# One read of w2 for two products, and V six items further behind K, in a two-block attention and MLP training step

## Chip, core and metric

The kernel runs on one core of a Trainium2 chip. The metric is the device time of one execution in microseconds (us). Engine names: PE does matmuls and transposes (PEld: its loads of the stationary operand), DVE, ACT and POOL work on vectors, SP issues the loads from memory. "arena" is the on-chip memory of the kernel, cut into twelve 1 MB slots and eight planes that hold the probabilities. For slots, blocks and slabs 1 MB is 2^20 bytes; in rates and read totals it is 10^6.

## The reference, cut to what matters

The model runs the same attention and the same MLP twice, then the gradients of all weights and of K and V are computed. There is one token, so all products with weights are matrix times vector, and the 64 MB each of K and V dominate.

```python
x = x + attn(layernorm(x), k_cache, v_cache, wq, wo)     # 32 heads, 4 KV groups, 65536 keys, 128 wide
x = x + mlp(layernorm(x), w1, b1, w2, b2)                # 1024 -> 3584 -> 1024, relu squared
x = x + attn(layernorm(x), k_cache, v_cache, wq, wo)
x = x + mlp(layernorm(x), w1, b1, w2, b2)                # its result is out_0
...                                                      # vjp: gradients of x, K, V, wq, wo, w1, b1, w2, b2
```

out_0 needs the second MLP's output product, h times w2. Nothing else in the step needs out_0: the gradients start from a given grad_out.

## The kernel before

The program has four passes over K and V and a short "dense stage" of weight products between each two of them.

| part | what it does | us in the profile before |
|---|---|---|
| first pass, second pass | attention forward: K, exponentials, V | to 374, and 424 to 773 |
| first dense stage | between them; reads w1 and w2 for the first MLP | 374 to 424 |
| second dense stage | second MLP without its output, gradient through w1 | 773 to 825 |
| third pass | gradient of the second attention, V leads and K follows | 825 to 1189 |
| third dense stage | dq to dx2 (wq), dx2 to dh2 (w2), dh2 to dx1 (w1), wo | 1189 to 1243 |
| fourth pass | gradient of the first attention, and all stores | 1243 to 2036 |

A pass goes through items of eight chunks of 128 keys, 256 items per pass. Four items are a block of 1 MB, which takes a slot. In a forward pass each step of the pipeline does K of one item and V of the item that lies FWD_LAG steps back:

```python
FWD_LAG = TLEAD + SU // 8 + 12            # 2 + 16 + 12 = 30 items
TOUCH = [touch_order(ITEMS[0], [("k", 0), ("v", FWD_LAG)]), ...]   # the order in which blocks are first needed
...
early_turn = set(k for k in TOUCH[p][:-2] if k in KV["keep"])      # V blocks turned in place for the third pass
...
pipeline(items, [(kT, 0), (kS, TLEAD), (v8, FWD_LAG)], bg, end, holds)
```

A block is loaded when it is first needed in program order; the load then waits on the chip until its slot is free.

The output product of the second MLP runs in the background of the third pass. The gradient product dx2 to dh2 reads the same w2 again in the third dense stage:

```python
bg.by_group(2, lambda g: g_dO(L3, dx3, g))
x4 = vec.tile([P, DC], F32, name="x4")
def g_out0():                              # out_0 = x3 + h @ w2 + b2, seven slabs of 1 MB
    yield from g_w2(L4, x3, x4, ps_bg)
    col_to_dram(x4, D, out_0.rearrange("a b d -> (a b d)"))
    yield
bg.add(g_out0())
... third pass ...
rows.add(PRE["wq3"], DC, R, lambda: L3["dqT"][:, gsl(lastg[2])], fin_dx2)
rows.add(w2_slabs()[0], FC, DC, lambda: dx2[:], fin_dh2, mix=True)      # w2 again
rows.add(w1_slabs()[0], DC, FC, lambda: dh2[:], fin_dx1, cols=f_cols, mix=True)
rows.add(wo_slabs(firstg[3])[0], R, DC, lambda: dx1[:], dO_finish(L1, firstg[3]))
rows.run()
```

Rows computes products whose vector runs along the rows of the stored weights. Each chunk of a slab is either turned on PE (eight transposes, L630), copied out of PSUM, and multiplied on PE (eight matmuls of 64 columns, L655), or it is multiplied and summed by one DVE instruction (L621). A balancer decides for each chunk, when the program is built, from running sums of the estimated load of PE, DVE and ACT.

## Time and profile before

The time is 2037.89 us (median of three runs, 2037.04 to 2039.66). First the profile page of the kernel before: the rate of the loads and stores in 40 slices of the span, and the bytes.

```profile
GB/s 389 424 417 418 420 423 404 362 357 420 420 418 403 419 415 278 382 419 408 421 419 421 411 334 245 370 399 424 421 418 423 391 424 400 358 392 424 424 397 247
HBM read 632.30 MB, written 165.69 MB: 392 GB/s over the span
```

In the middle of the first three passes most slices have 415 to 424 GB/s, and the deep dips there are the dense stages (slices 8 and 9, 16 and 17, 24 to 26). The Trainium skill, "Perfetto Trace Analysis", section Roofline, gives about 435 GB/s as what the 16 DMA engines of one core can move; 424 is 97% of it, and no slice of this trace goes above 424. So a byte less in a pass should be time.

The windows view of the kernel before shows the joints. The columns are the stretch in us, its length, each engine's busy us with the number of instructions, the granted PE clock, the DMA share and the rate.

```profile
core 0: us, PE busy (x) PEld busy (x) DVE busy (x) ACT busy (x) POOL busy (x), PEclk, DMA share, GB/s
745.00:774.00 29.00, 21.85 (x482) 21.15 (x479) 11.33 (x31) 19.36 (x38) 0.00 (x0) 0.88 0.82 328
1182.00:1245.00 63.00, 53.98 (x1049) 50.74 (x1045) 42.20 (x107) 34.66 (x40) 1.28 (x12) 0.92 0.86 323
1200.00:1216.70 16.70, 16.50 (x333) 15.97 (x333) 14.06 (x31) 12.43 (x14) 0.12 (x1) 0.90 0.79 289
```

The last line is the product dx2 to dh2. PE is busy for 16.50 of its 16.70 us: work added for PE here should lengthen it, unless it moves elsewhere. The granted clock of 0.90 stands for one stretch of 3.4 us at half clock inside it (1201.0 to 1204.4 us).

The PE timeline of the kernel before, at the end of the second pass (start, length, engine, line, operation, output and inputs, count, and in brackets the idle time before it with what ended it):

```profile
757.67 1.05 PE L1012 MATMUL ps_acc<-arena 128*128 128x64 bf16 x32
763.56 0.59 PE L1012 MATMUL ps_acc<-arena 128*128 128x64 bf16 x8 [4.84 <-ACT arena L993]
763.96 1.04 PE L1018 MATMUL ps_tr<-ident_b,arena 128*128 128x128 bf16 x8
```

PE has no V item left that could run and waits 4.84 us for the last exponentials. After that the eight transposes take 1.04 us. They take 0.61 us elsewhere.

The load queue of the kernel before at the start of the third pass. L330 is a single load, L335 the first load of 2 MB:

```profile
834.33 0.33 SPq L330 DMA_DIRECT2D arena<-in_A_v_cache_dram  x1
845.00 0.33 SPq L335 DMA_DIRECT2D arena<-in_A_k_cache_dram  x1
```

Nothing is issued for over 10 us. PE runs dry a little later (PE timeline, before):

```profile
853.06 0.61 PE L1147 MATMUL ps_acc<-dsT,arena 128*128 128x64 bf16 x8 [4.54 <-DMA arena<-in_A_k_cache_dram]
859.60 0.98 PE L1102 MATMUL ps_tr<-ident_b,arena 128*128 128x128 bf16 x8 [2.82 <-DMA arena<-in_A_v_cache_dram]
```

### The profile page before, as it was taken

To read this page: it belongs to the slowest core of one execution; us is meant where nothing else is said; L and a number is where in the kernel's file an instruction comes from. 1 tells how busy PE (TensorE), PEld (TensorE's weight loads), DVE (VectorE), ACT (ScalarE), POOL (GpSimd) and SP (SyncE) were. 2 spreads that over 40 slices of the span, in tenths; PEclk is the share of its full clock that TensorE was granted. 3 is DMA by queue.
4 is the path that set the end of the run, shared out by engine and by line. 5 is a ranking of instruction groups with operands and counts; after the bars stand their busy time and mean duration, and the time that the engine had idled before them with its cause. 6 is when DMAs were issued, how large, how long until landed. Compare 5 with 4: busy or idle time off the path is not lost. (4 is left out here: it accounts for less than half of the span.)

```text
span 2036.4 us, 67140 instructions
## 1 busy us (share of the span) xinstructions
PE 1630.6 (80%) x30274; PEld 1340.6 (66%) x30274; DVE 1175.9 (58%) x2355; ACT 1042.2 (51%) x1612; POOL 143.8 (7%) x328
## 2 busy tenths in 40 slices
PE   6878688688777877767777888788788888698896
PEld 6878688687777777767777786455455555455554
DVE  5645465245554644335444467577677777678675
ACT  3434344135343453235453446576676667567675
POOL 0000000000000000000000001111111111111121
PEclk9989898689998998889989999789888889789898
DMA  9999999999999997999999996999999999999996
GB/s 389 424 417 418 420 423 404 362 357 420 420 418 403 419 415 278 382 419 408 421 419 421 411 334 245 370 399 424 421 418 423 391 424 400 358 392 424 424 397 247
DMA packets 111981, 802.32 MB, mean 394 GB/s; under 512 B 9536, under 2 KB 9550, under 8 KB 49486
## 3 DMA queue, kind: packets, MB, share of 16 engines
q1 hardware_dynamic: 87646, 632.33, 76.4%
q0 software_dynamic: 24048, 165.70, 19.7%
q8 instruction: 236, 3.87, 0.7%
q14 instruction: 51, 0.42, 0.1%
HBM read 632.30 MB, written 165.69 MB: 392 GB/s over the span
## 5 line engine op out<-in xcount | busy, mean ns | idle before, releaser
L153 DVE COPY kt<-ps_tr 128x1024 bf16<-128x1024 bf16 x722 | 496.5, 689 | 455.3 <-PE ps_tr L910 223.7
L150 ACT CAST arena<-ps_gg 128x1024 bf16<-128x1024 f32 x452 | 439.8, 1010 | 220.5 <-PE ps_gg L1277 165.4
L910 PE MATMUL ps_tr<-ident_b,arena 128*128 128x128 bf16 x3840 | 310.7, 227 | 60.6 <-DMA arena<-in_A_k_cache_dram 46.6
L150 ACT COPY kt<-ps_tr 128x1024 bf16<-128x1024 bf16 x162 | 170.4, 1052 | 214.2 <-PE ps_tr L1102 152.1
L910 PEld LDWEIGHTS <-arena 128*128 128x128 bf16 x3840 | 234.2, 101 | 63.4 <-DMA arena<-in_A_k_cache_dram 49.8
L153 DVE CAST arena<-ps_gg 128x1024 bf16<-128x1024 f32 (+1 forms) x191 | 228.9, 1198 | 76.4 <-PE ps_gg L1277 42.5
L1012 PE MATMUL ps_acc<-arena 128*128 128x64 bf16 (+4 forms) x4096 | 209.5, 197 | 54.2 <-ACT arena L993 19.0
L1277 PE MATMUL ps_gg<-GG,xt 64*128 64x512 bf16 x1024 | 212.7, 414 | 42.9 <-DVE arena L153 22.2
L1223 PE MATMUL ps_tr<-ident_b,arena 128*128 128x128 bf16 x1824 | 178.1, 236 | 36.8 <-DMA arena<-in_A_v_cache_dram 36.0
L1012 PEld LDWEIGHTS <-arena 128*128 128x128 bf16 x4096 | 163.4, 101 | 59.4 <-issue 40.8
L928 PE MATMUL ps_sc<-L_qpad,kt 128*128 128x64 bf16 (+7 forms) x3584 | 183.8, 194 | 18.1 <-issue 17.9
L1102 PE MATMUL ps_tr<-ident_b,arena 128*128 128x128 bf16 x1888 | 157.0, 231 | 46.7 <-DMA arena<-in_A_v_cache_dram 44.9
L993 ACT ACTIVATE arena<-S_sb,L_negm 128x128 bf16<-128x128 f32 x256 | 165.1, 1002 | 55.1 <-DVE L_negm L978 45.9
L1223 PEld LDWEIGHTS <-arena 128*128 128x128 bf16 x1824 | 120.4, 105 | 93.1 <-issue 52.6
L928 PEld LDWEIGHTS <-kt 128*128 128x128 bf16 x3584 | 153.4, 100 | 21.0 <-issue 18.6
L1102 PEld LDWEIGHTS <-arena 128*128 128x128 bf16 x1888 | 119.2, 103 | 51.4 <-DMA arena<-in_A_v_cache_dram 48.0
L1303 PE MATMUL ps_acc<-X,arena 128*128 128x64 bf16 (+3 forms) x2048 | 121.3, 200 | 24.6 <-DMA arena<-in_A_k_cache_dram 24.6
L1303 PEld LDWEIGHTS <-arena 128*128 128x128 bf16 x2048 | 88.5, 103 | 60.0 <-issue 33.5
L993 ACT ACTIVATION_READ_ACCUMULATOR arena<-S_sb,L_negm 128x1 f32 x256 | 127.7, 499 | 0.0
L1256 PE MATMUL ps_sc<-DOB,kt 128*128 128x64 bf16 (+3 forms) x1824 | 118.0, 200 | 0.0
L1256 PEld LDWEIGHTS <-kt 128*128 128x128 bf16 x1824 | 85.7, 103 | 47.4 <-issue 45.9
L1277 PEld LDWEIGHTS <-xt 64*128 64x128 bf16 x1024 | 61.2, 94 | 82.9 <-issue 44.2
(264 smaller groups left out, 2197.4 us busy)
## 6 DMA issues: line engine op xcount, KB each, us to landing
arena<-in_A_k_cache_dram SPq DMA_DIRECT2D x86, 2048.0 KB, 20.1
arena<-in_A_v_cache_dram SPq DMA_DIRECT2D x82, 2048.0 KB, 18.7
out_dram<-arena POOLq DMA_DIRECT2D x151, 1024.0 KB, 11.3
arena<-in_A_v_cache_dram SPq DMA_DIRECT2D x78, 1024.0 KB, 16.3
arena<-in_A_k_cache_dram SPq DMA_DIRECT2D x76, 1024.0 KB, 11.4
arena<-in_B_w_dram SPq DMA_DIRECT2D x32, 896.0 KB, 6.7
arena<-in_B_w_dram SPq DMA_DIRECT2D x21, 1024.0 KB, 10.0
arena<-in_A_wq_dram SPq DMA_DIRECT2D x20, 1024.0 KB, 12.2
```

The costliest lines, as they stand in the source:

```text
L150: nc.scalar.copy(out=out, in_=in_)
L153: nc.vector.tensor_copy(out=out, in_=in_)
L910: nc.tensor.transpose(pt[:, i, :], kb8[:, i, :], ident_b[:, :])
L928: nc.tensor.matmul(state["ps_s"][:, s:s + w, :].rearrange("p a b -> p (a b)"), lhsT=kt[:, i, :], rhs=L["qpad"][:, g, 0:w, :].rearrange("p ...
L993: nc.scalar.activation(out=E(p, g, c0, SU)[:, :, h], in_=S[:, h, :], func=ACTF.Exp, bias=L["negm"][:, g, su, h:h + 1], scale=SCALE, accum_ ...
L1012: nc.tensor.matmul(ps_o[:, 0:w, :], lhsT=vb8[:, i, :], rhs=E(p, g, c, w), start=(c % SU == 0), stop=(c % SU == SU - 1), skip_group_check=True)
L1102: nc.tensor.transpose(pt[:, i, :], vb8[:, i, :], ident_b[:, :])
L1223: nc.tensor.transpose(pt[:, i, :], vb8[:, i, :], ident_b[:, :])
L1256: nc.tensor.matmul(state["ps_dp"][:, s:s + w, :].rearrange("p a b -> p (a b)"), lhsT=vt[:, i, :], rhs=DOB[:, g, 0:w, :].rearrange("p a b - ...
L1277: nc.tensor.matmul(pg[:, 512 * h:512 * h + 512], lhsT=xt[64 * h:64 * h + 64, j1 // 8 + m, :], rhs=gg[64 * h:64 * h + 64, :, :].rearrange(" ...
L1303: nc.tensor.matmul(ps_dq[:, 0:w, :].rearrange("p a b -> p (a b)"), lhsT=kb8[:, i, :], rhs=X[:, s:s + w, :].rearrange("p a b -> p (a b)"), ...
```

## The change

The output product of the second MLP moves from the third pass into the third dense stage, where it uses the w2 slabs that the gradient product loads anyway ("side"). One read of w2, 7.34 MB, disappears. V lags K by 36 items instead of 30, so that there is V left to do when the last exponentials are late. One more block is left out of the early turning of V at the end of the second pass.

```diff
-    FWD_LAG = TLEAD + SU // 8 + 12
+    FWD_LAG = TLEAD + SU // 8 + 18
...
                 for kc, slab in it:
+                    if job["side"] is not None:
+                        job["side"](kc, slab)
                     yield from self.front(job, kc, slab)
...
-        early_turn = set(k for k in TOUCH[p][:-2] if k in KV["keep"])
+        early_turn = set(k for k in TOUCH[p][:-3] if k in KV["keep"])
...
-    x4 = vec.tile([P, DC], F32, name="x4")
-
-    def g_out0():
-        yield from g_w2(L4, x3, x4, ps_bg)
-        col_to_dram(x4, D, out_0.rearrange("a b d -> (a b d)"))
-        yield
-    bg.add(g_out0())
...
-    rows.add(w2_slabs()[0], FC, DC, lambda: dx2[:], fin_dh2, mix=True)
+    x4 = vec.tile([P, DC], F32, name="x4")
+    ps_x4 = ps_acc([P, 64, DC])
+
+    def side_x4(kc, slab):
+        for nb in range(DC):
+            nc.tensor.matmul(ps_x4[:, :, nb], lhsT=d_cols(slab, nb), rhs=L4["gb"][:, kc:kc + 1].to_broadcast([P, 64]),
+                             start=kc == 0 and nb == 0, stop=kc == FC - 1 and nb == DC - 1, skip_group_check=True)
+        add_load(pe=DC * 0.03)
+        if kc == FC - 1:
+            f = tmp.tile([P, DC], F32, name="ffn_f")
+            nc.vector.tensor_tensor(out=f[:], in0=ps_x4[:, 0, :], in1=b2c[:], op=ALU.add)
+            nc.vector.tensor_tensor(out=x4[:], in0=x3[:], in1=f[:], op=ALU.add)
+            col_to_dram(x4, D, out_0.rearrange("a b d -> (a b d)"))
+    rows.add(w2_slabs()[0], FC, DC, lambda: dx2[:], fin_dh2, mix=True, side=side_x4)
```

More of the change, by code (lines that the diff above doesn't have):

```diff
@@ L576, in __init__, with add @@
             self.feed = None
-        def add(self, slab_it, nk, nj, vcol, finish, cols=d_cols, mix=False):
+        def add(self, slab_it, nk, nj, vcol, finish, cols=d_cols, mix=False, side=None):
             job = self.job(nk, nj, vcol, finish, cols, mix)
+            job["side"] = side
             self.jobs.append((slab_it, job))
@@ L584, in job @@
             pieces = [(k, min(8, nj - k)) for k in range(0, nj, 8)]
-            return dict(nk=nk, pieces=pieces, nj=nj, vcol=vcol, finish=finish, done=0, cols=cols, mix=mix, vbc=vbc, slot=None)
+            return dict(side=None, nk=nk, pieces=pieces, nj=nj, vcol=vcol, finish=finish, done=0, cols=cols, mix=mix, vbc=vbc, slot=None)
         def begin(self, job):
```

## The prediction

> **What bounds the kernel.** Mostly the DMA. The page's DMA row shows 9 in nearly all slices; in the middle of the passes the rate is 420 to 424 GB/s, and 802 MB in 2036 us is 394 GB/s on average. The Trainium skill, "Perfetto Trace Analysis", Roofline, puts a single core's ceiling at about 435 GB/s over its 16 DMA engines; the 424 of this trace agrees, so bytes are time there. PE's 80% busy is no limit in the passes. DMA time is lost at the joints: the windows view gives 351 GB/s for 376 to 431 us (first dense stage), 328 for 745 to 774 (end of the second pass), 326 for 774 to 827 (second dense stage), 323 for 1182 to 1245 (third). There chains of PE, ACT and DVE work decide.
>
> **What the change does.**
>
> 1. It removes one read of w2: 7 loads of 1 MiB, 7.34 MB, between 824 and 905 us, nearly all in the third pass, where the DMA runs at about 420 GB/s. Estimate: 7.34 MB / 424 GB/s = 17.3 us, all critical. The slabs also held arena slots: the load queue issues nothing from 834 to 845 us, and PE then waits 4.5 and 2.8 us for K and V (timeline, 853 and 860 us). I expect 2 us of that back.
>
> 2. It adds 224 matmuls of 64 columns to the third dense stage. Eight such take 0.23 us there (timeline): 28 x 0.23 = 6.5 us of PE. From 1201.5 to 1216.5 us PE has almost no idle time, and DVE and ACT are nearly full too, so little hides: some slabs go into the wait for dx2 (3 us of holes near 1200 us), and the balancer moves a few to DVE. With the output's short chain: +6 us.
>
> 3. V lagging K by 36 items instead of 30 fills PE at the joints. At the end of the second pass V waits 4.84 us for the last exponentials (timeline, 758.7 to 763.6 us; ACT L993), and the transposes after it take 1.04 us per eight instead of 0.61. That fits the Trainium skill, "TensorE: Matmul & The Clock Gate", Part 1: after an idle window the clock halves. Six more V items fit in that wait, and four items fewer are turned in the tail (0.45 us each): -4.5 us. At the start of the second pass PE waits 3.67 us (446 us), with the DMA at 260 GB/s: -2.5 us. At the end of the first pass the same wait is 3.75 us, but a DMA wait of 3.18 us follows: -1 us. The steady state does not change.
>
> Sum: -17.3 - 2 + 6 - 4.5 - 2.5 - 1 = -21 us. Held back a little, because gains at joints tend to be lost to the DMA behind them: **2018 us**, 8 in 10 within 2009 to 2028 us. Faster by over 2% (under 1997 us): 0.01; within 2%: 0.985; slower: 0.005.
>
> **What the profile would show.** Read bytes 625 instead of 632 MB. The third pass shorter by 17 to 20 us. The third dense stage longer by 4 to 8 us. The wait of L1012 for L993 at the end of the second pass under 2 us, and no half-speed transposes after it.
>
> **What would make it wrong.** The DMA in the third dense stage could hide the later matmuls, or the side products could stall PE on DVE for over 10 us. A longer lag leaves more V to load after the last K with few free slots; then the tails grow into DMA waits and point 3 turns into a loss.

## More of the kernel before

In the middle of the first three passes two neighbouring blocks go together into two adjacent slots as one load of 2 MB. The last eight blocks of a pass go singly, and so do the first ten of the second and third pass and all of the fourth:

```python
def take_pair():                           # the pair of adjacent free slots that was freed first
    both = [(max(FREE[i], FREE[i + 1]), i) for i in range(0, NG, 2) if i in FREE and i + 1 in FREE]
    ...
def kv8(t, g, c8):
    ...
    if NOW["pairs"] and hb % 2 == 0 and ... and key not in KV["halves"]:
        i = take_pair()
    if i is None:
        ...                                # L330: load of one 1 MB block
    else:
        ...                                # L335: load of 2 MB into slots i, i + 1
def start_pass(p):
    ...
    KV["halves"] = set(TOUCH[p][-8:] + (TOUCH[p][:10] if p else []))
```

## The result, and the profile after

The changed kernel took 2031.03 us (median of four runs, 2029.41 to 2034.35); the kernel before, in four runs, 2038.78 us. The ratio is 0.996, with a 95% interval of 0.9939 to 0.9982. In five rounds on another chip it was 0.9949 (0.9927 to 0.997). A ratio here is the mean time of one kernel's runs over that of the other's in the same rounds, so it is not quite the ratio of the medians. The gain is 8 to 11 us where the prediction expected 20, and the time lies above its range.

The page of the changed kernel:

```profile
GB/s 389 420 420 420 419 423 397 371 362 420 420 418 420 420 399 279 352 420 421 420 417 412 401 267 266 370 410 423 422 420 421 393 423 396 363 402 423 421 379 245
HBM read 624.96 MB, written 165.69 MB: 390 GB/s over the span
```

The bytes are 7.34 MB fewer, as they must be. The next table cuts several profiles into stages. "Last K" and "last V" are the starts of the last matmuls with K and with V of a pass. The third pass runs from the end of the second dense stage (its last row product) to the last fold of dq, the third dense stage from there to its last row product. Two profiles of the changed kernel, and two of the version with lag 30 that only shares the read (run below as share_only and share_again), show how far one profile can be trusted: about 2 us in a pass or in the third dense stage, 3.5 to 5 us in the time at which the second dense stage ends.

| us | before | lag 36 alone | share alone (two profiles) | changed (two profiles) |
|---|---|---|---|---|
| last K of the first pass at | 355.2 | 350.0 | 354.9 / 355.0 | 350.4 / 351.0 |
| last V of the first pass at | 374.2 | 374.0 | 373.8 / 373.5 | 374.0 / 373.7 |
| last K to last V, second pass | 22.3 | 21.9 | 22.0 / 22.0 | 21.7 / 21.7 |
| end of the second dense stage at | 825.2 | 817.9 | 824.1 / 820.6 | 824.4 / 819.4 |
| third pass | 364.1 | 366.5 | 345.1 / 346.5 | 349.6 / 349.5 |
| third dense stage | 53.9 | 50.8 | 59.2 / 60.4 | 60.6 / 60.3 |
| fourth pass to the end | 793.2 | 795.3 | 796.2 / 795.0 | 793.1 / 795.2 |

Two rows stand out. The third pass lost 14.5 us in the changed kernel, but 17.6 to 19.0 us in the version with the old lag. And the longer lag moved the last K of the first pass 4 to 5 us earlier, and its last V not at all.

The lines that answer to those of before come from the second profile of the changed kernel. The PE timeline at the end of its second pass:

```profile
757.67 1.05 PE L1015 MATMUL ps_acc<-arena 128*128 128x64 bf16 x32
759.07 0.39 PE L1015 MATMUL ps_acc<-arena 128*128 128x64 bf16 x8 [0.35 <-DVE zn L1037]
759.30 0.61 PE L1021 MATMUL ps_tr<-ident_b,arena 128*128 128x128 bf16 x8
```

The wait of 4.84 us is gone, and the transposes take 0.61 us. That part of the mechanism is as predicted. The wait of 3.67 us for the exponentials at the start of the second pass is gone too: neither profile of the changed kernel shows one from 430 to 480 us. Yet the tail from the last K to the last V takes 21.7 us, where it took 22.3.

The load queue of the changed kernel at the start of the third pass, and PE's wait:

```profile
823.98 0.33 SPq L330 DMA_DIRECT2D arena<-in_A_k_cache_dram  x1
825.11 0.33 SPq L330 DMA_DIRECT2D arena<-in_A_v_cache_dram  x1
837.41 0.33 SPq L335 DMA_DIRECT2D arena<-in_A_k_cache_dram  x1
```

```profile
846.90 0.61 PE L1150 MATMUL ps_acc<-dsT,arena 128*128 128x64 bf16 x8 [6.15 <-DMA arena<-in_A_k_cache_dram]
```

The standstill of the load queue was supposed to shrink with w2 gone. It is 12.3 us from one issue to the next; before it was 10.7.

The third dense stage: the PE timeline, changed kernel, and the windows view of its product dx2 to dh2.

```profile
1175.35 0.41 PE L656 MATMUL ps_bg<-vcb,wt 128*128 128x64 bf16 x8
1175.59 0.61 PE L1553 MATMUL ps_acc<-L_gb,arena 128*128 128x64 bf16 x8
1176.01 0.64 PE L631 MATMUL ps_tr<-ident_b,arena 128*128 128x128 bf16 x8
```

```profile
1181.50:1203.20 21.70, 21.68 (x442) 21.24 (x439) 16.42 (x37) 14.20 (x16) 0.79 (x3) 1.00 0.68 240
```

From start to start, eight row products (L656) take 0.24 us, and eight side products (L1553), of the same shape, 0.42 us. PE is busy for 21.68 of 21.70 us in a product that took 16.7 us before. The two ran at different granted clocks, 1.00 here and 0.90 before. In the profiles of lag_only and read3 (run below), which leave this product as it was, the clock over it is 1.00 and it takes 15.3 us, so at an equal clock the side products lengthened it by 6.4 us.

### The profile page after: what moved, and what is told of

It is laid out like the page before. It is cut to its first block, busy times and chain, and to the rows that moved or that the text cites. A ratio compares the mean times of both kernels' runs of the same rounds, so it can differ in the third digit from the quotient of the medians.

```text
span 2027.6 us, 67015 instructions
## 1 busy us (share of the span) xinstructions
PE 1626.9 (80%) x30210; PEld 1332.9 (66%) x30210; DVE 1174.3 (58%) x2358; ACT 1044.6 (52%) x1613; POOL 144.5 (7%) x332
## 5 line engine op out<-in xcount | busy, mean ns | idle before, releaser
L913 PE MATMUL ps_tr<-ident_b,arena 128*128 128x128 bf16 x3840 | 310.2, 226 | 60.4 <-DMA arena<-in_A_k_cache_dram 45.1
L931 PEld LDWEIGHTS <-kt 128*128 128x128 bf16 x3584 | 153.3, 100 | 23.6 <-issue 14.6
L1150 PE MATMUL ps_acc<-dsT,arena 128*128 128x64 bf16 (+7 forms) x2048 | 103.7, 195 | 20.0 <-DMA arena<-in_A_k_cache_dram 15.8
## 6 DMA issues: line engine op xcount, KB each, us to landing
out_dram<-arena POOLq DMA_DIRECT2D x151, 1024.0 KB, 11.4
```

The source lines that it names most:

```text
L913: nc.tensor.transpose(pt[:, i, :], kb8[:, i, :], ident_b[:, :])
L931: nc.tensor.matmul(state["ps_s"][:, s:s + w, :].rearrange("p a b -> p (a b)"), lhsT=kt[:, i, :], rhs=L["qpad"][:, g, 0:w, :].rearrange("p ...
L1150: nc.tensor.matmul(ps_dq[:, 0:w, :].rearrange("p a b -> p (a b)"), lhsT=kb8[:, i, :], rhs=dsT[:, s:s + w, :].rearrange("p a b -> p (a b)") ...
```

## The experiments

Theory: the read is worth what was predicted; the side product costs what was predicted in sum; the longer lag gains nothing, because its gains stop at the next load. Rivals: the read gives less than its bytes (its slabs went partly into idle DMA time), or the side product costs more than 6 us. Letters and numbers in the texts on record name the theories of that text alone. Where those texts speak of the stretch 20 to 40 us after the end of the second dense stage, I had read the transfers on a clock 10 us off; on the clock of this document it is 8 to 28 us after that end, with the same counts of MB.

### The two halves of the change apart

lag_only is the kernel before with `SU // 8 + 18` and `TOUCH[p][:-3]`:

> Only the longer lag of V (36 for 30 items, one block fewer turned early), w2 still read in the third pass. Theory A (the trace of after: V ends 5.8 us sooner at the end of the second pass, but the second dense stage ends only 0.7 us sooner, because the w1 loads there wait for slots): within 2 us of before, ratio 0.999 to 1.001; V of the second pass ends 4 to 7 us sooner, the dense stage after it grows by 4 to 6 us. Rival B (as predicted, the lag is worth 8 us and the loss lies in the w2 part): 6 to 10 us faster. Rival C (the lag costs): over 3 us slower.

Measured: 2037.11 us, ratio 0.9997 (0.9983 to 1.001). The lag alone is worth nothing. The time is what theory A said, but its profile does not show theory A's reason: the last V of the second pass came 8.7 us sooner, and the second dense stage grew by 1.4 us only, not by 4 to 6. (The profiled run, 2032.25 us, was the fastest of the six.)

share_only is the changed kernel with `SU // 8 + 12` and `TOUCH[p][:-2]`. It was run again later on another chip, beside versions below, as share_again:

> Only the shared read of w2, the lag as before (30). Theory A: 6 to 9 us faster than before, so all of the change's gain, third pass 14 to 18 us shorter and the third dense stage 6 to 7 us longer. Rival B (the lag holds the gain of the pair): 0 to 2 us faster. Rival C: over 10 us faster, because the lag was a loss.

> The shared read with the old lag once more (lag 30, first 10 blocks single), as the reference of these rounds: 2028 to 2032 us, third pass 345 to 346 us.

Measured: 0.9967 (0.9954 to 0.9979), 2031.02 us, and 0.9948 (0.9926 to 0.997), 2028.53 us. The changed kernel itself was run again too:

> The changed kernel once more, in the same rounds as the others, as their reference. 2028 to 2033 us; the third pass again 348 to 350 us from the end of the second dense stage to its last dq, with 5.0 to 5.4 MB moved in the stretch from 20 to 40 us after that end.

Measured: 0.9949 (0.9927 to 0.997), 2027.84 us. So all of the change's gain comes from sharing the read.

### What the read is worth

read0 is the kernel before without the output product, and read3 with three of its seven slabs. Their outputs are wrong, which doesn't matter for the times.

```diff
-        yield from g_w2(L4, x3, x4, ps_bg)
+        nc.vector.tensor_copy(out=x4[:], in_=x3[:])      # read0; read3 runs the product over 12 of 28 chunks
+        yield
```

> Before with the last product of the second block left out altogether (out_0 is wrong on purpose): no read of w2 in the third pass and no side products later. Theory A1 (bytes alone, 7.34 MB at 424 GB/s): 17 us faster than before. Theory A2 (three of the seven slabs were issued at 814, 817 and 824 us, in the joint where the DMA has idle time, so only four cost): 10 to 13 us faster.

> Before with three of the seven w2 slabs read and multiplied (out_0 wrong on purpose). Theory A1 (every byte costs the same): 4/7 of what read0 gains, 9 to 10 us faster than before, 7 us slower than read0. Theory A2 (the first three slabs ride in idle DMA time of the joint): as fast as read0 within 2 us, 10 to 13 us faster than before.

Measured: read0 0.9914 (0.9897 to 0.993), 17.8 us less in the mean; read3 0.9953 (0.9941 to 0.9965), 9.8 us less. Taking out four slabs of seven gives 9.8 of 17.8 us, which is 0.55 where 4/7 is 0.57: the time goes with the bytes. The prediction's 17.3 us fits, though the interval of read0 is wide (14 to 21 us). The rival that the slabs of the joint are free falls.

### What the side product costs

few_side is the changed kernel with the side product of the first and last chunk only (wrong), few_side_lag30 the same with lag 30.

```diff
-        for nb in range(DC):
+        for nb in range(DC) if kc in (0, FC - 1) else ():
```

> After with the side products of 26 of the 28 chunks left out (out_0 wrong on purpose), everything else as after. Theory A (208 matmuls in a stage where PE is the limit cost 7 to 11 us, more than the 6 predicted: the first seven stand in front of dx2 and lengthen that wait by 2.8 us, the rest lengthen dx2 to dh2 by 5): 8 to 11 us faster than after, so 2020 to 2023 us, and the stage from the last dq of the third pass to dh2 falls from 35.7 to about 28 us. Rival B (the product costs no more than the predicted 6 us): 2025 us or more.

> share_again without 26 of the 28 chunks of the side product (out_0 wrong on purpose). If the side product costs what the traces of its stage show (5 to 7 us): 5 to 7 us faster than share_again. If it costs the 11 us by which read0 and share_only differ: 10 to 12 us faster.

Measured: few_side 0.993 (0.9911 to 0.9949), few_side_lag30 0.9922 (0.99 to 0.9944). In the same rounds share_again is 5.3 us slower than few_side_lag30 (mean differences to before of 10.7 and 16.0 us). few_side itself is 4 us faster than the changed kernel (0.9949, other rounds), where 8 to 11 were expected. A second measure: read0 and share_only, in the same rounds, differ by 9.8 us (17.8 and 8.0), and both lack the second read of w2. read0 lacks the whole side product, with its output chain in the third dense stage; the few_side kernels keep the chain, two chunks, and the balancer's load estimates. So the side product costs between 4 and 10 us, and with intervals of 4 to 6 us each way (estimated from those of the ratios) the runs do not say where between. The product dx2 to dh2 takes 17.0 us in both, at a granted clock of 0.90, against 21.7 us with the side products, at 1.00. The windows view of few_side over it:

```profile
1181.60:1198.60 17.00, 15.00 (x281) 14.15 (x282) 15.42 (x35) 11.66 (x13) 0.15 (x2) 0.90 0.65 237
```

Not everything in these two profiles is clear: the next product, dh2 to dx1, took 26.4 and 24.2 us where the kernels with side products have 22.6 and 22.2 (the clock explains part of it for few_side at most: 0.87 over that product, 0.92 to 0.93 in the other three), and the third pass of few_side_lag30 took 342.5 us although its program up to there is that of share_again (346.5). The run times are the better measure here.

defer holds back the side products of up to three slabs until dx2 is there (the seven that stand before dx2 lengthen the wait for it by 2 to 3 us), and defer_bal also tells the balancer of 3 us of PE work at the start:

```diff
+    wait = []
     def side_x4(kc, slab):
+        wait.append((kc, slab))
+        if dx2_done or len(wait) == 12:
+            while wait:
+                one_x4(*wait.pop(0))          # the body of before; a slab is freed once its chunks are done
```

> After with the side products of the first slabs kept back until dx2 is worked out (their slabs are freed later); the same matmuls, another order. If seven side products in front of dx2 lie on the chain, the last dq to dx2 falls from 14.0 to 11 us and the kernel is 2 to 3 us faster than after (2028 us). Rival: they only move the same PE work behind dx2, or the later freed slabs delay w2, and the time stays within 1 us of after.

> defer, and the balancer starts this job with 3 us of PE load, so that two or three slabs more go to DVE (which in after ends 5 us before PE). Expected: dx2 to dh2 falls from 21.7 to about 19.5 us, 1.5 to 2 us faster than defer. If DVE was not idle in truth, no faster than defer.

Measured: defer 0.995 (0.9933 to 0.9967), defer_bal 0.9942 (0.9925 to 0.9959). Neither differs from the changed kernel's 0.9949. The side products in front of dx2 were not worth moving: what dq to dx2 gains in defer (12.3 us, against 14.1 and 12.7 in the changed kernel), dx2 to dh2 gives back (23.6 us). In defer_bal dx2 to dh2 takes 21.7 us, where 19.5 were expected.

coltile turns the product round. The vector's column is the stationary operand, 1 wide, and w2 streams 512 columns, on four column tiles of the PE array, so there are 56 matmuls in place of 224, and 8 small ones to add the four partial rows.

```diff
-            nc.tensor.matmul(ps_x4[:, :, nb], lhsT=d_cols(slab, nb), rhs=L4["gb"][:, kc:kc + 1].to_broadcast([P, 64]), ...)
+        for k, sl in wait4:                   # four chunks, two halves of 512 columns each
+            for h in range(2):
+                c = 32 * (2 * (k % 2) + h)
+                nc.tensor.matmul(ps_row[c:c + 1, :], lhsT=L4["gb"][:, k:k + 1], rhs=sl[:, 512 * h:512 * h + 512], ...,
+                                 tile_position=(0, c))
```

> After with the output product turned round: the activation column is the stationary operand, w2 streams as 512 columns, on four column tiles at once, 56 matmuls for 224, and eight small ones to sum up. If the four column tiles run side by side, the product costs about 56 x 0.21 / 4 = 3 us of PE for 6.6, and the kernel is 2 to 4 us faster than after. If they run one after the other (56 x 0.21 = 12 us), it is 4 to 7 us slower than after.

> coltile with the old lag of V (30, two blocks not turned). If the lag is worth nothing while the slot gap stands: within 1.5 us of coltile (2026 us), third pass 345 to 346 us for 349. If the lag is worth its 2 to 4 us: slower than coltile by that.

The PE timeline of coltile, in the third dense stage:

```profile
1185.97 0.60 PE L1564 MATMUL ps_acc<-arena,L_gb 128*1 128x512 bf16 x8
1186.51 0.62 PE L631 MATMUL ps_tr<-ident_b,arena 128*128 128x128 bf16 x8
```

A slab takes 0.54 us of PE, where the side product takes 4 x 0.42 = 1.68 us. Among the eight, the starts lie 3 to 4 ns apart within four, then about 205 ns: four run side by side, as the Trainium skill, "TensorEngine Tiling (Array Packing)", section Tiling Modes, has it for 128x32 tiles (four tiles). Measured: coltile 0.9933 (0.9913 to 0.9952), coltile_lag30 0.9924 (0.9903 to 0.9945). Against the changed kernel's 0.9949 and share_again's 0.9948 that is 3 to 5 us in the middle, with intervals that overlap.

### Where the lag's gain went

The longer lag does end the second dense stage earlier: at 821.2 us on average over the twelve profiles with lag 36 (817.9 to 824.4), at 823.3 over the eight with lag 30 (820.2 to 825.7). That is 2.2 us (before rounding) of the 8 predicted. The last V of the second pass comes 3.8 us earlier in the same profiles (766.2 and 770.0), so the second dense stage keeps 1.6 us of that. In the third pass it is lost again. Slots are assigned when the program is built, so this can be followed in the program's own bookkeeping, without a chip. The first load of 2 MB takes the pair of adjacent slots that was freed first:

| | first pair of slots | freed, in steps after the pass began |
|---|---|---|
| before | 6, 7 | 21, 25 |
| share alone, lag 30 | 0, 1 | 15, 16 |
| changed, lag 36 | 8, 9 | 24, 16 |

With lag 36 the last V blocks of the second pass fall into other slots, and no two neighbours are free before step 24, though slots 1, 3 and 9, of three different pairs, were free by step 16. SP issues the loads in program order, so the loads behind it wait as well. The load queue of share_again:

```profile
827.63 0.33 SPq L330 DMA_DIRECT2D arena<-in_A_v_cache_dram  x1
833.33 0.33 SPq L335 DMA_DIRECT2D arena<-in_A_k_cache_dram  x1
838.40 0.33 SPq L335 DMA_DIRECT2D arena<-in_A_v_cache_dram  x1
```

The standstill is 5.7 us there. It belongs to the program and not to one run: it is 12.3 us in all seven profiles that share the read with lag 36 and load the first ten blocks singly, and 5.7 to 5.9 us in the five with lag 30 that do not read w2 in the third pass. With the second read of w2 it is 10.7 us at lag 30 and 12.8 us at lag 36 (lag_only). A test: let more of the first blocks of the third pass be loaded singly, so that no adjacent pair is needed so early. halves18 does this in the changed kernel, halves18_lag30 in share_only:

```diff
-        KV["halves"] = set(TOUCH[p][-8:] + (TOUCH[p][:10] if p else []))
+        KV["halves"] = set(TOUCH[p][-8:] + (TOUCH[p][:18 if p == 2 else 10] if p else []))
```

> After with the first 18 blocks of the third pass loaded as single megabytes instead of the first 10; nothing else. Theory A (with a lag of 36 the first load of a pair of adjacent slots in the third pass asks for a pair whose second half is given back some 20 items later than with a lag of 30, so the load queue stands still for 12 us): the gap in the load queue goes, 6.5 MB or more move from 20 to 40 us after the dense stage for 5.2, the third pass is 3 to 4 us shorter, and the kernel is 2 to 4 us faster than after_again. Rival B (the hole is set by other things: freed slots in general): third pass within 1 us of after.

> halves18 (lag 36) in the same rounds: 2020 to 2023 us. Theory A: 2 us faster than halves18_lag30. Rival B: equal to it.

> Shared read, old lag, first 18 blocks of the third pass single. Theory A (the lag gains about 2 us at the joints and had lost about 4 in the third pass through the late pair; single loads take that loss away): third pass 343 us as in halves18, kernel 2 us slower than halves18_again, and only 1 to 3 us faster than share_again, since with lag 30 there was less to win. Rival B (the lag gains nothing even without the gap): equal to halves18_again within 1 us.

The load queue of halves18 in the same stretch:

```profile
825.37 0.33 SPq L330 DMA_DIRECT2D arena<-in_A_v_cache_dram  x1
828.49 0.33 SPq L330 DMA_DIRECT2D arena<-in_A_k_cache_dram  x1
831.68 0.33 SPq L330 DMA_DIRECT2D arena<-in_A_v_cache_dram  x1
832.61 0.33 SPq L330 DMA_DIRECT2D arena<-in_A_k_cache_dram  x1
```

The windows view of the 20 us from about 8 us after the end of the second dense stage, of the kernels before, share_again, the changed kernel and halves18, in this order:

```profile
833.00:853.00 20.00, 14.73 (x415) 13.63 (x412) 5.51 (x9) 3.62 (x4) 0.00 (x0) 1.00 0.82 328
```

```profile
829.00:849.00 20.00, 15.51 (x405) 14.40 (x402) 9.91 (x17) 12.62 (x20) 0.00 (x0) 0.97 0.93 360
```

```profile
827.00:847.00 20.00, 13.85 (x361) 12.62 (x359) 9.50 (x16) 8.97 (x14) 0.00 (x0) 0.95 0.69 273
```

```profile
828.00:848.00 20.00, 18.04 (x466) 16.65 (x464) 11.54 (x21) 12.47 (x20) 0.00 (x0) 1.00 1.01 416
```

Over these 20 us the rate goes from 273 GB/s in the changed kernel to 416 GB/s, the PE wait of 6.15 us is gone, and the third pass takes 343.2 and 342.3 us in the two profiles with lag 36. Measured: halves18 0.9923 (0.9905 to 0.9942), in the same rounds in which the changed kernel had 0.9949, and halves18_again 0.9923 (0.9902 to 0.9945). The third pass is 6 to 7 us shorter, the kernel 5 us in the middle of the intervals. halves18_lag30 has 0.9939 (0.9921 to 0.9957) beside share_again's 0.9948: about 2 us in the middle, where less standstill was there to remove. Its third pass fell to 342.3 us as well, but its later stages were some 5 us longer in the profile than share_again's. dh2 to dx1 took 25.4 us there at a granted clock of 0.80, against 22.2 at 0.92; for 3.8 us in the fourth pass I have no reason. Only with this repair does the lag look useful: lag 36 and 30 in the same rounds are 0.9923 and 0.9939, with intervals that overlap.

best18 joins coltile and halves18:

> coltile and halves18 together, lag 36: the gains should add, 3 to 5 us from coltile and 2 to 4 us from the load gap, so 2022 to 2025 us, 13 to 16 us faster than before. If both work on the same wait, no faster than coltile.

Measured: 0.9913 (0.9892 to 0.9935), 2021.07 us. In the same rounds that is 2 us less than halves18, where coltile_lag30 and coltile had given 3 to 5 us: the runs do not show that the two gains add up.

### Why eight side products take 0.42 us

Both L656 and L1553 have 64 moving columns. L1553 writes its 64 results into every eighth column of its PSUM tile, L656 into neighbouring ones. contig changes the layout alone, contig_halves18 does it in halves18:

```diff
-    ps_x4 = ps_acc([P, 64, DC])
+    ps_x4 = ps_acc([P, DC, 64])
...
-            nc.tensor.matmul(ps_x4[:, :, nb], lhsT=...
+            nc.tensor.matmul(ps_x4[:, nb, :], lhsT=...
...
-            ... in0=ps_x4[:, 0, :] ...
+            ... in0=ps_x4[:, :, 0] ...
```

> The changed kernel with the side product's PSUM tile laid out [128, 8, 64] instead of [128, 64, 8], so each matmul of 64 columns writes 64 neighbouring columns instead of every eighth; nothing else moves. Theory S (the strided write is why these eight take 0.42 us where eight row products of the same 64 columns take 0.23): the side product's start to start falls to 0.23 to 0.26 us per eight, PE of the third dense stage falls by 28 x 0.18 = 5 us, the stage is 2 to 4 us shorter, ratio to the kernel before 0.993 to 0.994 where the changed kernel had 0.995. Rival T (the pace has another cause, such as the stationary columns coming from a loaded slab rather than from a transposed tile): still 0.40 to 0.43 us per eight and the same time as the changed kernel within 0.1%.

> The same layout in the version whose first 18 blocks of the third pass are loaded one MB at a time (which had 0.9923 twice). Theory S: 0.23 to 0.26 us per eight, stage 2 to 4 us shorter, ratio 0.990 to 0.9915. Rival T: 0.42 us per eight, ratio 0.992 to 0.993. Both theories expect the same 8 MB in the 20 us behind the second dense stage and a third pass of 342 to 344 us.

The PE timeline of contig:

```profile
1177.54 0.41 PE L1553 MATMUL ps_acc<-L_gb,arena 128*128 128x64 bf16 x8
1177.79 0.61 PE L631 MATMUL ps_tr<-ident_b,arena 128*128 128x128 bf16 x8
```

Eight side products now take 0.25 us from start to start. The groups of the changed kernel and of contig show the sum (busy us, mean ns of one, idle before):

```profile
L1553 PE MATMUL ps_acc<-L_gb,arena 128*128 128x64 bf16 x224 | 15.5, 246 | 0.0
```

```profile
L1553 PE MATMUL ps_acc<-L_gb,arena 128*128 128x64 bf16 x224 | 9.9, 193 | 0.0
```

So the strided write was the cause: about 55 ns per matmul, from start to start, became 31. The Trainium skill, "TensorE: Matmul & The Clock Gate", Part 1, section "Wait — 56ns, not 53.3ns?", gives a warm start-to-start time of columns / 2.4 GHz plus about 2.5 ns, from which I estimate 29 ns for 64 columns. The row products and contig, at 31 ns, come close; the strided form takes as long per matmul as the transposes of 128 columns do in the same stage (56 ns).

The time did not follow: contig 0.9951 (0.9935 to 0.9968), the same as the changed kernel. The product dx2 to dh2 still takes 22.0 us. The windows view and three lines of the PE timeline of contig suggest why:

```profile
1182.90:1204.90 22.00, 19.43 (x430) 18.88 (x430) 16.27 (x38) 14.52 (x16) 0.82 (x4) 0.92 0.68 241
```

```profile
1198.64 0.27 PE L190 MATMUL ps_mv<-ident_f,x 128*8 128x128 f32 x1 [2.10 <-DVE x L1559]
1199.09 1.04 PE L631 MATMUL ps_tr<-ident_b,arena 128*128 128x128 bf16 x8
1199.92 0.63 PE L656 MATMUL ps_bg<-vcb,wt 128*128 128x64 bf16 x8
```

PE is no longer full, 19.43 of 22.00 us. It waits 2.10 us for x4, the finished output: the two DVE instructions that compute it stand behind eleven DVE row products, one after the other from 1185.6 to 1198.2 us. PE's next transposes stand behind the transpose of x4. After the wait PE ran at half clock for 3.4 us (1198.9 to 1202.3 us; eight transposes took 1.04 us instead of 0.61), which the changed kernel did not do in this product (clock 1.00). So the wait and the clock after it took back most of what the layout gave; that the order of the instructions is the limit now was not tested by a run. contig_halves18 has 0.9914 (0.9898 to 0.9931), 2021.21 us; halves18 had 0.9923, so the layout is worth at most a few us there, and the intervals do not tell.

## Why the prediction was right and wrong

**The read (point 1) was right.** Predicted 17.3 us for the bytes and 2 for the freed slots; read0 measured 17.8 for both together, in proportion to the bytes (read3). Of the 2 us little or nothing shows even with lag 30 (the third pass lost 17.6 to 19.0 us); with lag 36 part of the 17.3 was lost as well (14.5 us).

**The side product (point 2) is not settled in sum, and two errors in it partly cancelled.** Predicted +6 us; the runs put it between 4 and 10 us (few_side and few_side_lag30; read0 and share_only). The third dense stage grew by 6.4 to 6.7 us against the one profile of before, but by 9.5 to 9.8 us against lag_only, which had no stretch of half clock there. That the first number is so near 6 is partly luck. The single cost was taken from row products with a neighbouring write, 0.23 us per eight, and it was 0.42, so PE had 28 x 0.42 = 11.8 us to do rather than 6.5. And more was hidden than I allowed: the balancer gave DVE 11 row products of dx2 to dh2 where it had 7 before, and some slabs ran while PE waited for dx2.

**The lag (point 3) was wrong, and it is the step that failed.** It was to give 4.5 + 2.5 + 1 = 8 us, and lag_only shows 0.9 of 2038 us, within the noise; with sharing, lag 36 and lag 30 are equal (0.9949 and 0.9948).

- At the end of the first pass I expected 1 us. The last K came 4 to 5 us sooner, the last V at the same time. V then waits for its loads, as these lines of the PE timelines show; the old wait for the exponentials has turned into a wait for DMA. The first two lines are from before, the third from the changed kernel:

```profile
363.98 2.96 PE L1012 MATMUL ps_acc<-arena 128*128 128x64 bf16 x64 [3.75 <-ACT arena L993]
370.12 1.89 PE L1012 MATMUL ps_acc<-arena 128*128 128x64 bf16 x32 [3.18 <-DMA arena<-in_A_v_cache_dram]
369.69 1.89 PE L1015 MATMUL ps_acc<-arena 128*128 128x64 bf16 x32 [6.07 <-DMA arena<-in_A_v_cache_dram]
```

- At the end of the second pass the wait of 4.84 us and the slow transposes did vanish. But the tail still takes 22 us, since six more items of V lie between the last K and the last V. All that a longer lag can gain is that K ends sooner. At the end of the second dense stage 2.2 us of the 7 predicted up to there (4.5 and 2.5) are left, as a mean over twenty profiles, each group of which scatters over 5 to 7 us.
- "The steady state does not change" was the sentence that failed most. The lag changes the order in which blocks are first needed, hence which slots come free, hence when the first adjacent pair does. The standstill at the start of the third pass went to 12.3 us where share_again has 5.7, and the third pass is about 4 us longer: 349 to 350 us in seven profiles, 344.5 to 346.5 in four of the five with lag 30 and no w2 in the third pass (few_side_lag30 has 342.5). That eats the 2 us and the hoped-for relief of point 1. halves18 shows that the standstill is the cause of this part: without it the third pass is 6 to 7 us shorter, and as long with lag 36 (342.3 and 343.2 us) as with lag 30 (342.3, halves18_lag30).

With measured terms the sum is -17.8 + 5.3 + 0 = -12.5 us, or -8.0 us with the 9.8 us by which read0 and share_only differ. The runs gave -8.1 and -11.4 us. So the lag's 8 us are the part of the miss that the runs show; the side product may hold up to 4 us more. The prediction had named the loss ("gains at joints tend to be lost to the DMA behind them"; a longer lag may turn tails into DMA waits), but it took only about 1 us off for it (a sum of 21 us, 20 in the time), where 8 were due.

Two readings of the prediction were taken on the shifted clock named above: the w2 loads were issued from 814 to 878 us rather than between 824 and 905, and the windows view gives 292 GB/s, not 260, for the 16 us from 424 us. Neither carries the argument.

**Open:** the profiles of one program differ by up to 5 us in where a stage ends, so the small items above are means. What the side product costs is known only as 4 to 10 us. Whether best18, contig_halves18 and halves18 differ is not settled; they lie at 0.9913, 0.9914 and 0.9923. Whether contig gains once the output's short chain is moved behind the row products was not tried. No version was slower than before, and the best ones take 2021 to 2023 us, 16 to 18 us less than before; the smallest edit that gets there is the change with halves18.

## What to carry to other kernels

When a kernel is bound by loads, as this one is, bytes removed are worth their time at the measured rate. A deeper pipeline lag only moved the wait to the next load here; what it can gain depends on whether the load can start sooner as well. Before calling a reordering neutral, replay the program's buffer assignment: an in-order load queue stops at the first load whose buffers are late, and a 2 MB load that needs two neighbours can be later than two singles. Take the cost of a matmul from one with the same output stride, and when an engine is relieved, look at once for the instruction order that may hold it next. Compare stages of two profiles only with the granted clock beside them.

## What the Trainium skill lacked or had wrong

- The formula for the start-to-start time in Part 1 of "TensorE: Matmul & The Clock Gate" has no term for the layout of the output. "PSUM — Partial Sum Buffer", Specifications (TRN2), does say that a non-contiguous access pattern slows matmuls significantly, but no page that was found says by how much. With the output written to every eighth fp32 column of PSUM, 64-column matmuls started every 55 ns or so, and every 31 ns once the same results were written to neighbouring columns (contig).
- Part 1 of the same page has the clock drop to half after an idle window of about 3.4 us. The wait of 4.84 us fits: transposes took 1.04 us per eight after it, and 0.61 us without it. But in contig a wait of 2.10 us was followed by half clock as well (1.04 us per eight), so here the clock halved after a shorter wait than the page names.
- No page that was found works through loads issued in order that all wait behind one whose buffer is late. Here that made the difference between 273 and 416 GB/s over 20 us (the changed kernel and halves18).
